# Attention operands and small sums rearranged between VectorE, ScalarE and GpSimd in a fused attention, MoE and FFN kernel

## The chip, the cores and the metric

The kernel runs on one core of one Trainium2 chip. The time is device microseconds of that core for one launch. A core has TensorE (PE, matmuls; its weight loads are shown as PEld), VectorE (DVE), ScalarE (ACT), GpSimd (POOL), SyncE (SP, which only issues transfers here) and 16 DMA engines. PE writes to PSUM; POOL works on SBUF alone.

## The reference, cut to what matters

Attention with a linear memory for B = 4 batches, H = 8 heads, S = 576 tokens and head size D = 64; its output feeds a top-1 mixture of 8 experts and then a dense FFN with ELU.

```python
scores = scale * (q @ k.T), causal, minus the row's maximum
a = exp(scores);  a /= a.sum(-1, keepdims=True) + 1e-9
local = a @ v
q_p = where(q > 0, q, exp(q) - 1) + 1
mem_out = (q_p @ M_prev) / ((q_p @ z_prev) + 1e-6)
g = 1 / (1 + exp(-beta))                       # one number per head
attn = g * mem_out + (1 - g) * local
logits = attn @ w_gate + modality_bias[modality_id]   # 2304 tokens x 8 experts
x = gate_w * (relu(attn @ w1[e]) @ w2[e])             # e: the expert with the largest logit
out = elu(x @ w_in) @ w_out
```

## The kernel before

The program is written against a tile framework: the order of the instructions on each engine is written out by hand, and the framework puts in the waits between engines from what each instruction reads and writes.

**Attention.** The 32 heads are done as 16 pairs p (four pairs a batch). A pair has NU = 7 units (L393): k = 0 is the last 64 tokens of both heads, k = 1 to 6 are tiles of 128 query rows of one head (two small tiles together in the last two units). For each unit, `scores` (L402) does the matmuls and a DVE pass (`low`, L399) that scales, masks and takes the row's minimum; one unit later `weights` (L437) takes the exponential on ACT (L447) with the row sum as a side result in `SUM[p]`; three units later PE transposes (`transposes`, L470), four later `evacuate` copies to SBUF (L482 on DVE, L480 on ACT). In unit 4 of the next pair come the products with V (`pv`, L507), `pv_tail` (L514, L515) and copies on ACT (L516, L517, L520). Two pairs on, in unit 0, `back` (L539) multiplies the result, which stands with head size on partitions, by the matrix `RH`: an identity for each head of the pair beside that head's rows of w_gate, so that one matmul turns the tile back to rows of tokens and gives its share of the gate's logits.

**Precision.** The score matmuls split q and k into a rounded high part and a low rest. `heads` holds three operands per pair. `prep_a` (L372, ACT) writes the rounded copy of q and of k to all 128 partitions; q and k were loaded twice, to partitions 0 to 63 and 64 to 127. `prep_b` (POOL) writes L = q - high (L378, 128 partitions) and overwrites one half of K, partitions 64 to 127, with k - high (L380). So K is [high; low] over the 128 contracted rows, Q is [high; high], and two matmuls, Q K and L K (L428, L429), give all four products. They are put for the next pair in units 0, 1, 3 and 4 (`PRE`): L378, L380, L378, L380, on POOL in that order with `fin` between.

**Small sums.** `tail_sums` (L529, DVE, unit 3) spreads the last tile's row sums over two columns with a mask `halves`; a small matmul in `pv_tail` gathers them. `row_scales` (L543, unit 5 of the next pair) makes (1 - g) / (sum + 1e-9) in three DVE steps (L548, L549, L550). `scaled` (L557) multiplies the output of `back` by it, `mem` (L581 to L583) does the memory part, and `fin` (L608, POOL; L606 on DVE from pair FINV = 13 on) adds the two: four adds a pair, of which two, for the last 64 tokens, are on partitions 0 to 63 for even batches and 64 to 127 for odd ones. The sums of the gate's part go to LX and LT.

**The order on DVE.** Small DVE steps do not stand in the written order. They lie in two queues, `steps` and `slow`; `pump` (L355), called behind each of the larger DVE instructions (L399, L482, L385, L389), takes one from `steps` and advances `slow` once. `drain` empties `steps` ahead of `back` and `mem`. Routing of a batch (`logits`, `route_a` to `route_c`, L611 to L714) lies in `slow`: it starts at pair 5, 9 and 13 for batches 0 to 2, with L614, which sums LX over the heads. The routed positions are scattered to a table in DRAM by POOL's indirect DMAs (`route_d`, L716, with the helper of L91 and L92), one per tile of 128 tokens, put at unit 4 of a later pair. Behind the third batch's scatters SP loads the first expert's indices (L897), POOL gathers its rows (L899), and the experts begin.

`omg` is 1 - g per head (L333), made by a `slow` step in pair 0. `mem_gate` (L313, units 0 and 1 of pair 1) multiplies the memory by the w_gate columns of RH.

Of the kernel before, what the change touches and what calls it, by code (L numbers as in the profile page):

```python
# [10 lines left out]
F32 = mybir.dt.float32  # L11
# [3 lines left out]
AF = mybir.ActivationFunctionType  # L15
ALU = mybir.AluOpType
# [12 lines left out]
DL = D + E  # L29
# [25 lines left out]
FINV = 13  # L55
# [47 lines left out]
def attention_memory_moe_ffn_kernel(  # L103
# [82 lines left out]
    with tc.tile_pool(name="ps", bufs=2, space=PSUM) as ps, ExitStack() as keep:  # L186
        for tag, n in (("s", 3), ("t", 2), ("po", 1), ("d", 2)):
            setattr(G, tag, lambda nm, tag=tag, n=n: ps.tile([128, 512], F32, tag=tag, bufs=n, name=nm))
        G.kp = keep.enter_context(G.pool("keep"))
        define_experts(tc, G)  # L190
        with G.pool("att") as ap, G.pool("hd", "right") as hd:
            attention(tc, G, ap, hd)
        ypool = ctx.enter_context(G.pool("yp", "right"))
        G.y = ypool.tile([128, 4, YW], F32, name="y")
        with G.pool("moe") as mp:
            experts(tc, G, mp)
# [4 lines left out]
def attention(tc, G, ap, hd):  # L201
    nc, wk = tc.nc, G.wk
# [11 lines left out]
    mm0, mod64, mt, lt0, halves = [k2[:, a:b] for a, b in ((0, 720), (720, 848), (848, 912), (912, 976), (976, 978))]  # L214
# [17 lines left out]
    RH = k1[:, o : o + 8 * DL].rearrange("p (k j d) -> p k j d", k=4, j=2)  # L232
# [51 lines left out]
    omg = ct("omg", [128, H])  # L284
# [39 lines left out]
            nc.vector.tensor_tensor(bd[r, :, j, D + 1 :].rearrange("p (b k) e -> p b k e", b=B), d[r, :, j].rearrange("p (b k) e -> p b k e", b=B), gj.unsqueeze(1).unsqueeze(3).to_broadcast([64, B, H // 2, E]), op=ALU.mult)  # L324


    def small_consts():
        nc.scalar.activation(g, bt, AF.Exp, scale=-1.0)
        nc.vector.tensor_scalar(g, g, 1.0, None, op0=ALU.add)
        yield  # L330
        nc.vector.reciprocal(g, g)
        yield
        nc.vector.tensor_scalar(omg, g, -1.0, 1.0, op0=ALU.mult, op1=ALU.add)  # L333
        yield
        for b in range(B):
            for j in range(2):
                r = slice(64 * j, 64 * j + 64)
                m = bd[r, 4 * b : 4 * b + 4, j, 1 : D + 1]
                nc.gpsimd.tensor_tensor(m, m, g[r].rearrange("p (h j) -> p h j", j=2)[:, :, j].unsqueeze(2).to_broadcast([64, H // 2, 64]), op=ALU.mult)
                yield  # L340
        nc.vector.tensor_copy(midf, mids.bitcast(I32).rearrange("p (t w) -> p t w", w=2))
        yield
        for m, dst in ((0, bm), (1, bm1)):
            nc.vector.tensor_scalar(midf[:, :, 1], midf[:, :, 0], float(m), None, op0=ALU.is_equal)
            yield
            nc.vector.tensor_tensor(dst, midf[:, :, 1:2].to_broadcast([128, NT, E]), mbs[:, m : m + 1, :].to_broadcast([128, NT, E]), op=ALU.mult)
            yield
        nc.vector.tensor_tensor(bm, bm, bm1, op=ALU.add)
        yield


    steps, slow = deque(), deque()
# [15 lines left out]
    def ops_of(p):  # L368
        return heads[:, p % 2, 0], heads[:, p % 2, 1], heads[:, p % 2, 2]
# [4 lines left out]
    def prep_b(p, j, r, eng=nc.gpsimd):  # L374
        qd, kd = LDT[p % 2][0:2]
        Q, K, L = ops_of(p)
        if r == 0:
            eng.tensor_tensor(L[:, j], qd[:, j, 0:512], Q[:, j].bitcast(F32), op=ALU.subtract)  # L378
        else:
            eng.tensor_tensor(K[64:128, j], kd[64:128, j, 0:512], K[64:128, j].bitcast(F32), op=ALU.subtract)  # L380

    def prep_phi(p, r):
        q2, m = LDT[p % 2][2], QP[p % 2]
# [11 lines left out]
    SRT, MX, SUM, ST = {}, {}, {}, {}  # L395
# [129 lines left out]
    STL = {}  # L525

    def tail_sums(p):
        STL[p] = wk.tile([128, 2], F32, tag="st", name=f"st{p}")
        nc.vector.tensor_tensor(STL[p], SUM[p][:, 4, 0:1].to_broadcast([128, 2]), halves, op=ALU.mult)  # L529

    def back(p):
        b = p // 4
# [8 lines left out]
    RS = {}  # L541

    def row_scales(p):  # L543
        h0 = 2 * (p % 4)
        rs = RS[p] = wk.tile([128, 5, 2], F32, tag="rs", name=f"rs{p}")
        steps.extend(
            (
                lambda: nc.vector.tensor_scalar(rs, SUM[p], 1e-9, None, op0=ALU.add),  # L548
                lambda: nc.vector.reciprocal(rs, rs),  # L549
                lambda: nc.vector.tensor_tensor(rs, rs, omg[:, h0 : h0 + 2].unsqueeze(1).to_broadcast([128, 5, 2]), op=ALU.mult),  # L550
            )
        )

    def scaled(p, d, a0, a1):
        k = a1 - a0
# [3 lines left out]
    def head_end(p):  # L559
        steps.extendleft(  # L560
            (
                lambda: fin(p),
                lambda: scaled(p, DB[p], 3, 5),
                lambda: scaled(p, DA[p], 0, 3),
            )
        )
# [20 lines left out]
    def fin(p):  # L587
        b, hp = p // 4, p % 4
        xs, xt = XS[b % 2], XT[b // 2]
        if hp == 0:  # L590
            nc.gpsimd.memset(xs[:, :, DM + 1 : ROW], 0.0)
            if b % 2 == 0:
                nc.gpsimd.memset(xt[:, DM + 1 : ROW], 0.0)
        c0 = 128 * hp
        mm, ol = MM[p % 2], OL[p % 2]
        r = 64 * (b % 2)
        hs = slice(2 * hp, 2 * hp + 2)
        half = slice(r, r + 64)
        for out, rows, c, d in (
            (xs[:, :, c0 : c0 + 128].rearrange("p c (j d) -> p c j d", d=64), slice(0, 128), slice(0, 4), slice(0, D)),  # L600
            (xt[half, c0 : c0 + 128].rearrange("p (j d) -> p j d", d=64), half, 4, slice(0, D)),
            (LX[:, :, hs], slice(0, 128), slice(0, 4), slice(D, DL)),
            (LT[b // 2][half, hs], half, 4, slice(D, DL)),
        ):
            if p >= FINV:
                steps.append(lambda out=out, rows=rows, c=c, d=d: nc.vector.tensor_tensor(out, mm[rows, c, :, d], ol[rows, c, :, d], op=ALU.add))  # L606
            else:
                nc.gpsimd.tensor_tensor(out, mm[rows, c, :, d], ol[rows, c, :, d], op=ALU.add)  # L608
# [158 lines left out]
    def put(p, k, f, *a):  # L767
        beside.setdefault(NU * p + k, []).append((f, a))

    for p in range(NP):  # L770
# [12 lines left out]
        else:  # L783
            put(p, ML[0], mem, p, 0, 3, s)
            put(p, ML[1], mem, p, 3, 5, s)
        put(p, 3, tail_sums, p)
        put(p + 1, RSC, row_scales, p)
        put(p + 2, 0, back, p)
        put(p + 2, 0, head_end, p)
        put(p, PHI, prep_phi, p, 0)  # L790
        put(p, PHI + 1, prep_phi, p, 1)
        if p + 1 < NP:
            for n, (j, r) in enumerate(((0, 0), (0, 1), (1, 0), (1, 1))):
                k = PRE[n] if p else PRE0[n]
                put(p, k, prep_a, p + 1, j, r)
                put(p, k, prep_b, p + 1, j, r)
            put(p, 6, loadv, p + 1)
# [5 lines left out]
    for n, k in enumerate(MW):  # L803
        put(0, k, mem_gate, n)
    put(0, SMALL, slow.append, small_consts())
    put(1, 3, G.late_constants)
    for b in range(3):
        K = 4 + b % 2
        ts = [tile_of(b, c) for c in range(K)]
        p, k = 4 * b + 5, GK[b]  # L810
# [38 lines left out]
    def first_prep(j):  # L849
        for r in range(2):  # L850
            prep_a(0, j, r, nc.vector if r else nc.scalar)
            prep_b(0, j, r, nc.vector if r else nc.gpsimd)
# [632 lines left out]
```

## Time and profile before

| | us |
|---|---|
| three runs | 1003.69, 1004.15, 1006.15 |
| median | 1004.15 |
| the profiled execution | 1004.68 |
| its span, first to last instruction | 1003.0 |
| busy: PE, DVE, ACT, POOL | 890.0, 577.5, 494.2, 319.8 |

Times in the rows are from the start of the span. The attention ends near 270 us, the experts run to about 580 us, the FFN to the end. An instruction's duration on DVE or POOL includes time in which it has started but is held; PE's ends are modelled.

### The profile page before, as it was taken

Reading aid. Unit: us, or ns where it says so; the run is one execution under the profiler, and the core shown is the slowest. Engines: PE = TensorE matmul, PEld = TensorE weight load, DVE = VectorE, ACT = ScalarE, POOL = GpSimd, SP = SyncE. Lnnn points to the kernel's source line nnn. Section 1 sums busy time; section 2 is a strip of 40 time slices with the busy share of each in tenths; the row PEclk is TensorE's granted clock in tenths of the full one; section 3 lists DMA queues with packets and bytes.
Section 4 is the critical chain, followed back from the end, with each engine's and each line's share of the span. In section 5 each row is a group of like instructions: output and inputs, shape, how many; then the busy total and the mean of one; then the engine's idle time right before and its main releaser. Section 6 shows DMA issues by size and latency. Waiting matters only on the chain. (4 is left out here: it accounts for less than half of the span.)

```text
span 1003.0 us, 16466 instructions
## 1 busy us (share of the span) xinstructions
PE 890.0 (89%) x5944; PEld 793.7 (79%) x5944; DVE 577.5 (58%) x1363; ACT 494.2 (49%) x1136; POOL 319.8 (32%) x428
## 2 busy tenths in 40 slices
PE   7999797887656799979998669999999999999996
PEld 4777675666556699979998468999999999999995
DVE  6999886878565332234222359888654444644442
ACT  4777574665521221123221346666665566755553
POOL 5765464355334521000000023222232222322223
PEclk9999998998978899979999779999999999999998
DMA  9755374561815541024101024432010000100001
GB/s 207 183 135 143 83 187 74 137 140 65 181 35 156 57 167 46 22 61 149 29 24 24 26 88 137 157 126 85 1 64 1 1 1 1 64 1 1 1 1 64
DMA packets 34054, 78.30 MB, mean 78 GB/s; under 512 B 11536, under 2 KB 11664, under 8 KB 33936
## 3 DMA queue, kind: packets, MB, share of 16 engines
q1 hardware_dynamic: 28016, 62.61, 24.2%
q0 software_dynamic: 4832, 12.14, 3.9%
q10 hardware_dynamic: 1088, 2.10, 0.9%
q8 instruction: 60, 0.98, 0.5%
q14 instruction: 58, 0.48, 0.2%
HBM read 67.25 MB, written 9.58 MB: 77 GB/s over the span
## 5 line engine op out<-in xcount | busy, mean ns | idle before, releaser
L1339 POOL TENSOR_TENSOR gl<-eg,gh 128x384 fp32r<-128x384 f32 x86 | 94.2, 1095 | 275.5 <-PE fh L1320 187.1
L1350 PE MATMUL facc<-wl,gh 128*128 128x512 f32 x288 | 113.0, 392 | 1.0 <-POOL wl L1300 1.0
L1350 PE MATMUL facc<-wh,gl 128*128 128x512 f32 x288 | 113.2, 393 | 0.0
L1350 PE MATMUL facc<-wh,gh 128*128 128x512 f32 x288 | 112.0, 389 | 0.0
L940 PE MATMUL h<-xh,W 128*128 128x256 f32 x512 | 97.6, 293 | 15.4 <-issue 6.9
L959 PE MATMUL acc<-hs,W 128*128 128x256 f32 x864 | 107.0, 283 | 0.5 <-DVE xb L914 0.3
L1320 PE MATMUL fh<-yh,first_w 128*128 128x384 f32 x384 | 101.1, 345 | 6.7 <-ACT yh L1311 6.7
L959 PEld LDWEIGHTS acc<-hs,W 128*128 128x128 f32 x864 | 104.5, 190 | 0.8 <-DVE xb L914 0.5
L1327 ACT ACTIVATE er<-fh 128x384 f32<-128x384 f32 x96 | 47.2, 492 | 114.8 <-PE fh L1320 111.1
L1330 DVE SCALAR_TENSOR_TENSOR ee<-ee,er 128x384 f32<-128x384 f32 x48 | 27.9, 580 | 120.8 <-ACT er L1329 119.2
L940 PEld LDWEIGHTS h<-xh,W 128*128 128x128 f32 x512 | 83.2, 199 | 16.8 <-DVE hs L943 7.3
L899 POOL DMA_INDIRECT xb<-xd,gi x26 | 25.0, 960 | 201.5 <-ACT xh L924 78.6
L942 ACT ACTIVATE hs<-h 128x256 fp32r<-128x256 f32 x72 | 27.1, 384 | 106.3 <-PE h L940 84.7
L1320 PEld LDWEIGHTS fh<-yh,first_w 128*128 128x128 f32 x384 | 72.0, 193 | 9.0 <-ACT yh L1311 7.0
L940 PE MATMUL h<-xl,W 128*128 128x256 f32 x256 | 74.6, 291 | 0.0
L447 ACT ACTIVATE sr<-sr,mx 128x512 f32<-128x512 f32 (+3 forms) x96 | 53.7, 563 | 40.7 <-DVE mx L399 35.8
L943 DVE SCALAR_TENSOR_TENSOR hs<-h,hs 128x256 fp32r<-128x256 f32 x72 | 29.8, 422 | 63.5 <-ACT hs L942 62.5
L1320 PE MATMUL fh<-yh,wh 128*128 128x384 f32 x192 | 64.5, 336 | 0.9 <-DVE eg L1331 0.9
L1320 PE MATMUL fh<-yh,wl 128*128 128x384 f32 x192 | 64.4, 336 | 0.0
L1350 PEld LDWEIGHTS facc<-wl,gh 128*128 128x128 f32 x288 | 54.0, 188 | 11.7 <-POOL wl L1300 1.4
L482 DVE COPY aT<-t 128x512 f32<-128x512 f32 (+3 forms) x106 | 50.6, 485 | 22.1 <-PE t L470 22.0
L1350 PEld LDWEIGHTS facc<-wh,gl 128*128 128x128 f32 x288 | 54.0, 188 | 11.4
(348 smaller groups left out, 2170.2 us busy)
## 6 DMA issues: line engine op xcount, KB each, us to landing
lqk<-in_qk_dram SPq DMA_DIRECT2D x30, 576.0 KB
raw<-in_w_dram SPq DMA_DIRECT2D x20, 512.0 KB
fraw<-in_win_dram SPq DMA_DIRECT2D x14, 512.0 KB
fraw<-in_wout_dram SPq DMA_DIRECT2D x14, 512.0 KB
lq<-in_qT_dram SPq DMA_DIRECT2D x16, 320.0 KB
vt<-in_vP_dram SPq DMA_DIRECT2D x16, 320.0 KB
xd<-early_rows SPq DMA_DIRECT2D x2, 1032.0 KB
xd<-late_rows SPq DMA_DIRECT2D x2, 1032.0 KB
```

Of the source, the lines that this page charges most:

```text
L447: nc.scalar.activation(sr[:, o : o + W], sr[:, o : o + W], AF.Exp, scale=-1.0, bias=mx[:, r : r + 1], accum_out=SUM[p][:, i, j : j + 1])
L482: nc.vector.tensor_copy(dst, src)
L899: nc.gpsimd.indirect_dma_start(xb[:, h, :], None, xd[0:rows, :], bass.IndirectOffsetOnAxis(ap=gi[:, h : h + 1], axis=0))
L940: nc.tensor.matmul(hp, wt[:, k, 128 * f : 128 * f + 128], xt[:, k, :], start=(k == 0 and r == 0), stop=(k == 3 and r == 2))
L942: nc.scalar.activation(hh, hp, AF.Relu)
L943: nc.vector.scalar_tensor_tensor(hl, hp, 0.0, hh.bitcast(F32), op0=ALU.max, op1=ALU.subtract)
L959: nc.tensor.matmul(o, wt[:, f, 128 * dc : 128 * dc + 128], ht, start=(f == 0 and r == 0), stop=(f == FF // 128 - 1 and r == 2))
L1320: nc.tensor.matmul(hp, wt[:, k, :], xt[:, k, :], start=(k == 0 and r == 0), stop=(k == 3 and r == 2))
L1327: nc.scalar.activation(r, hp, AF.Relu, scale=-1.0)
L1330: nc.vector.scalar_tensor_tensor(e, e, 1.0, r, op0=ALU.add, op1=ALU.mult)
L1339: eng.tensor_tensor(gl, gg, gh.bitcast(F32), op=ALU.subtract)
L1350: nc.tensor.matmul(ACC[g][a], gt[:, c], wt, start=(f == 0 and r == 0), stop=(f == NF - 1 and r == 2))
```

## The change

K's low part goes to partitions 0 to 63, so that K is [low; high]; the matmuls are the same. The factor 1 - g is multiplied into RH once (`scale_rows`, in pair 1, unit 2) and no longer into the row scales. The tail sums and the addition of 1e-9 are ACT instructions in the written order, and only the reciprocal stays a DVE step. `fin`'s two adds on partitions 64 to 127 go to DVE steps for all pairs.

```diff
+    def scale_rows():
+        for j in range(2):
+            r = slice(64 * j, 64 * j + 64)
+            w = omg[r].rearrange("p (k j) -> p k j", j=2)[:, :, j].unsqueeze(2).to_broadcast([64, 4, DL])
+            nc.vector.tensor_tensor(RH[r, :, j], RH[r, :, j], w, op=ALU.mult)
...
-            eng.tensor_tensor(K[64:128, j], kd[64:128, j, 0:512], K[64:128, j].bitcast(F32), op=ALU.subtract)
+            eng.tensor_tensor(K[0:64, j], kd[0:64, j, 0:512], K[0:64, j].bitcast(F32), op=ALU.subtract)
...
-        nc.vector.tensor_tensor(STL[p], SUM[p][:, 4, 0:1].to_broadcast([128, 2]), halves, op=ALU.mult)
+        nc.scalar.activation(STL[p], halves, AF.Copy, scale=SUM[p][:, 4, 0:1])
...
     def row_scales(p):
-        h0 = 2 * (p % 4)
         rs = RS[p] = wk.tile([128, 5, 2], F32, tag="rs", name=f"rs{p}")
-        steps.extend(
-            (
-                lambda: nc.vector.tensor_scalar(rs, SUM[p], 1e-9, None, op0=ALU.add),
-                lambda: nc.vector.reciprocal(rs, rs),
-                lambda: nc.vector.tensor_tensor(rs, rs, omg[:, h0 : h0 + 2].unsqueeze(1).to_broadcast([128, 5, 2]), op=ALU.mult),
-            )
-        )
+        nc.scalar.activation(rs, SUM[p], AF.Copy, bias=1e-9)
+        steps.append(lambda: nc.vector.reciprocal(rs, rs))
...
-            if p >= FINV:
+            if p >= FINV or rows.start:
                 steps.append(lambda out=out, rows=rows, c=c, d=d: nc.vector.tensor_tensor(out, mm[rows, c, :, d], ol[rows, c, :, d], op=ALU.add))
...
+    put(1, 2, scale_rows)
```

## Rows read from the trace of the kernel before

**Rows 1.** Windows of 20 us: length; busy (count) of PE, PEld, DVE, ACT, POOL; clock; DMA
```profile
60.00:80.00 20.00, 19.25 (x184) 15.08 (x180) 18.21 (x56) 13.84 (x41) 10.08 (x10) 1.00 0.46 113
...
160.00:180.00 20.00, 13.80 (x106) 10.96 (x106) 15.81 (x52) 10.41 (x30) 12.37 (x17) 0.83 0.41 99
```

**Rows 2.** DVE's groups by line and shape, 0 to 340 us: busy us, mean ns
```profile
L529 DVE TENSOR_TENSOR st<-sum,small 128x2 f32<-128x2 f32 x16 | 13.5, 844 | 0.0
...
L548 DVE TENSOR_SCALAR rs<-sum 128x10 f32<-128x10 f32 x16 | 10.2, 636 | 0.0
...
L557 DVE TENSOR_TENSOR ol<-db,rs 128x288 f32<-128x288 f32 x16 | 7.2, 452 | 0.0
...
L550 DVE TENSOR_TENSOR rs<-rs,omg 128x10 f32<-128x10 f32 x16 | 4.5, 284 | 0.0
...
L549 DVE RECIPROCAL rs<-rs 128x10 f32<-128x10 f32 x16 | 3.2, 201 | 0.0
...
L674 DVE TENSOR_TENSOR r_rb<-r_rb,r_ps 128x8 f32<-128x8 f32 x18 | 2.9, 163 | 0.3
...
L606 DVE TENSOR_TENSOR late_rows<-mm,ol 64x128 f32<-64x128 f32 x2 | 0.6, 290 | 0.0
```

**Rows 3.** Timeline of one pair, 60 to 75 us: start us, us, engine, line
```profile
63.90 1.87 POOL L380 TENSOR_TENSOR heads<-lqk,heads 64x512 fp32r<-64x512 f32 x1 [3.48 <-ACT heads L372]
64.16 0.21 ACT L447 ACTIVATION_READ_ACCUMULATOR sr<-sr,mx 128x1 f32 x1
...
64.56 1.24 DVE L548 TENSOR_SCALAR rs<-sum 128x10 f32<-128x10 f32 x1
...
66.54 0.52 PE L470 MATMUL t<-ident,sr 128*128 128x128 f32 x3
...
68.05 0.55 DVE L482 COPY aT<-t 128x384 f32<-128x384 f32 x1
...
71.11 1.27 POOL L608 TENSOR_TENSOR early_rows<-small,ol 128x512 f32<-128x512 f32 x1
...
71.75 0.18 DVE L582 RECIPROCAL rn<-rn 128x6 f32<-128x6 f32 x1
...
72.81 1.69 DVE L529 TENSOR_TENSOR st<-sum,small 128x2 f32<-128x2 f32 x1
...
73.21 1.27 POOL L378 TENSOR_TENSOR heads<-lqk,heads 128x512 fp32r<-128x512 f32 x1
```

**Rows 4.** Waits, 0 to 340 us: total us, times, longest us
```profile
ACT sr L447 <- DVE mx L399: 35.8, 25, 5.8
...
DVE aT L482 <- PE t L470: 22.0, 16, 2.4
```

**Rows 5.** Timeline of POOL behind the scatters of the first and second batch
```profile
147.38 0.96 POOL L92 DMA_INDIRECT idreg<-tid,rpi  x1 [0.22 <-issue]
148.40 1.27 POOL L378 TENSOR_TENSOR heads<-lqk,heads 128x512 fp32r<-128x512 f32 x1
158.93 1.26 POOL L380 TENSOR_TENSOR heads<-lqk,heads 64x512 fp32r<-64x512 f32 x1 [9.26 <-DMA idreg<-tid,rpi]
...
226.15 1.27 POOL L380 TENSOR_TENSOR heads<-lqk,heads 64x512 fp32r<-64x512 f32 x1 [7.45 <-DVE rs L548]
```

**Rows 6.** Timeline of DVE in the two stalls
```profile
162.49 0.61 DVE L614 TENSOR_REDUCE lg<-late_rows 128x32 f32<-128x256 f32 x1 [5.05 <-POOL late_rows L608]
...
164.56 0.94 DVE L619 TENSOR_TENSOR lg<-lg,bm 128x40 f32<-128x40 f32 x1
...
229.47 0.61 DVE L614 TENSOR_REDUCE lg<-late_rows 128x32 f32<-128x256 f32 x1 [2.62 <-POOL late_rows L608]
```

**Rows 7.** ACT's groups by line and shape, 0 to 340 us: busy us, mean ns
```profile
L517 ACT COPY sum<-pt 128x2 f32<-128x2 f32 x16 | 2.7, 166 | 0.0
...
L328 ACT ACTIVATE g<-bt 128x8 f32<-128x8 f32 x1 | 0.2, 205 | 0.0
```

**Rows 8.** Waits of SP's own queue, 100 to 300 us: total us, times, longest us
```profile
SPq L897 <- DMA idreg<-tid,rpi: 18.6, 1, 18.6
```

## The prediction

> **What bounds the kernel now.** All edits lie in the attention stage, about the first quarter of the span, so I went past the shares of the whole span to windows of 20 us [rows 1]: from 60 to 80 us VectorE (DVE) is busy 18.21 of 20 us and TensorE (PE) 19.25; from 160 to 180 both fall, to 15.81 and 13.80. Busy does not mean working, and the groups by line show it [rows 2]: a DVE multiply of 128x2 elements (L529) takes 844 ns on average and an add on 128x10 (L548) 636 ns, while a reciprocal on the same 128x10 takes 201 ns. The timeline tells why [rows 3]: L529 starts at 72.81 and ends at 74.50, and POOL's L378 runs 73.21 to 74.48; L548 runs 64.56 to 65.80, POOL's L380 63.90 to 65.77. DVE's multiplies and adds with both inputs in SBUF, and its tensor_scalar from SBUF, are held until the running POOL instruction is over. The reciprocal L582 ran its 0.18 us inside POOL's L608 (71.11 to 72.38), so it is not held.
>
> What a held instruction costs depends on the place. L529 stands ahead of the stretch where PE does the previous pair's attention-times-V (L507). DVE catches up with PE once in each pair: `DVE aT L482 <- PE t L470` is 22.0 us in 16 waits [rows 4], and L529 is the last long DVE instruction ahead of it. L529 is thus under PE's cover. L548 comes right behind that catching-up, where DVE leads and TensorE and ScalarE wait for it (ScalarE 35.8 us in 25 waits [rows 4]): its 1.24 us are bare.
>
> The second thing is two stalls. Behind the idreg scatters of a batch, L378 (all 128 partitions) starts 0.06 us after the last scatter (147.38 + 0.96, then 148.40), but the next L380, on partitions 64 to 127, starts 9.26 us after L378 ended, and 7.45 us in the next batch [rows 5]. The first is put down to the landing of the scatters. The second is put down to DVE's L548, whose data L380 does not touch; it is the same place in the order, so I read it as the same wait, its last instant held by DVE, as DVE is by POOL above. In both, POOL's later adds (L608) come late, and DVE, which reduces what they write (L614), idles 5.05 and 2.62 us [rows 6]. L378 and L380 subtract the same kind of data of the same pair; what sets them apart is the partition they begin at. I read it so: the program orders a POOL instruction that begins at partition 64 behind all that POOL issued before, its DMAs included, and one from partition 0 not.
>
> **The change part by part.** The sum is made against the profiled execution, 1004.68 us (span 1003.0 and 1.7 around it), 0.5 above the median of the runs, 1004.15.
>
> *K as [low; high].* L380 has the same 64x512 shape on partitions 0 to 63; both take 1.26 to 1.27 when nothing is in the way [rows 5], so nothing there. What it removes is the two stalls. No POOL instruction from partition 64 on is then left behind a scatter, since the odd batches' adds leave POOL as well. DVE's 5.05 + 2.62 = 7.7 us go. In the first stall's wake a small add, L619, took 0.94 [rows 6], held by POOL's backlog, where an add of 128x8 takes 0.16 [rows 2]: 0.8 us more. Bounds: nothing (the wait is for something else) and 16.7, both of POOL's stalls whole (POOL itself leads).
>
> The Trainium skill speaks against this edit (Perfetto Trace Analysis, "GPSIMD Engine Instruction" and "DMA Instruction — SWDGE (GPSIMD)"): POOL is eight processors of 16 partitions each, each with a queue of its own, and numbers 0 and 1 build the scatters' descriptors. By this rule the new L380 would stand behind descriptor building and the old one would not. The row on L378, which uses all partitions and starts 0.06 us behind a scatter, does not show it; what the rule would make of the time is the first rival.
>
> *1 - g in the output matrix.* L550 goes: 16 times, 4.5 us [rows 2], bare like L548, for it follows two DVE instructions behind. Added is scale_rows once, two 64x288 multiplies: nearest row 128x288 at 452 ns [rows 2], 0.9 together; bounds 0.6 (two of 290 ns, 64x128) and 3.4 (each also held for a POOL instruction of 1.27). It must follow mem_gate's matmuls, but mem_gate's own DVE multiplies, just ahead of it, wait for the same matmuls. The output matmuls keep shape and number.
>
> *The add of 1e-9 on ScalarE.* L548 goes from DVE: 10.2 us [rows 2]. What is held behind L389 next? Copies from PSUM and the reciprocal, which POOL does not hold, so the wait does not move on. ScalarE gets 16 instructions between 166 ns (128x2) and 205 ns (128x8) [rows 7], 3 us in all, in a queue with room (13.84 of 20 busy [rows 1]). The wait added is the reciprocal's on ScalarE; behind it in DVE stand the score passes L399. ScalarE's slot is behind the L447 that ends at 64.37, so the add ends near 64.57; DVE would reach the reciprocal where L548 starts now, at 64.56 [rows 3]. That is no wait, but a close thing: 0, bounds 0 and 0.5 per pair, 8 in all.
>
> *Tail sums on ScalarE.* L529 goes: 13.5 us of DVE [rows 2], under PE's cover: I take 0. Much of the wait would move on as well: L385, next to read SBUF alone, would meet the same POOL instruction. Bounds 0 and 13.5. ScalarE's 16 new instructions, 3 us, use a value that ScalarE wrote itself.
>
> *Odd batches' tail adds on DVE.* Five pairs (4 to 7 and 12), two adds each, 64x128 at 290 ns and 64x16 near the 163 ns of a 128x8 add [rows 2]: 2.3 us. Both have two SBUF inputs and stand right behind fin's large POOL add (1.27 us [rows 3]), so they are held: from nothing to twice 1.27 per pair. I take 0.5 us per pair, since in three of the five pairs a routing step is held at that place already and they only take its turn: 2.3 + 2.5 = 4.8, bounds 2.3 and 15. POOL saves two small adds a pair, hidden under its own waits for ScalarE.
>
> Of L548 and L550, 14.7 us, not all reaches the end. In the pair shown DVE would be 1.4 us early, and its copy at 68.05 would come at 66.65, but PE's transposes for it start at 66.54 and take 0.52, to 67.06 [rows 3], behind PE's own work: 0.4 of 1.4 is lost. I keep 80%, 11.8; bounds 0 and 14.7.
>
> Sum: 11.8 + 7.7 + 0.8 - 0.9 - 4.8 = 14.6 us. Behind the attention the third batch's scatters start the chain that opens the expert stage: SyncE waits 18.6 us for their landing to load the indices [rows 8]. They are issued by DVE's pace, so all that follows moves up whole. 1004.7 - 14.6 = 990.1, and 989.5 against the median.
>
> **The rivals.**
> 1. *The stall stays.* L380 waits for the scatters for another reason than its partitions, or the low half's processors are busy with the descriptors until the landing. For it: the row names the landing. Against: L378, just ahead, does not wait. 8.5 us are lost: 998.6. The skill's rule of the two processors, above, ends here.
> 2. *PE covers all.* DVE's savings only lengthen its waits for PE, which is busy 19.25 of 20 us at 60 to 80 [rows 1]. Then 8.5 - 5.7 = 2.8 remain: 1001.9. Against: ScalarE's 35.8 us of waits for DVE [rows 4].
> 3. *L529 counts too.* If PE's stretch itself moves up and the wait does not pass to L385, up to 13.5 more: 976 to 985.
> 4. *Slower: the reciprocal waits for ScalarE.* The add is queued behind ScalarE's exponentials; if ScalarE comes late by w in each pair, DVE stands for 16w at L549. From w = 14.6 / 16 = 0.91 us the gain is gone; if ScalarE is late in each pair by as much as POOL is now at L548, 1.24 us [rows 3], the time is 1004.7 - 14.6 + 19.8 = 1009.9. Against: the two meet at 64.57 and 64.56, above, and ScalarE is idle a third of the time [rows 1].
>
> **How the numbers follow.** Forecast (985 to 994) 52%; rival 3, 20%; rival 1 (994 to 1000) 13%; rival 2 (1000 to 1003) 8%; rival 4, 5%; the remaining 2% are nothing at all. A difference under 0.3%, 3 us, can't be told from none here. Faster by more (under 1001.1): 52 + 20 + 13 + half of rival 2 = 89%; same 6%; slower 5%. The range 976 to 998.5 leaves out the tail of rival 1 and rivals 2 and 4.
>
> **What would show it.** In the changed profile L380's longest wait behind a scatter is ScalarE's copy and not idreg; L614's idle time goes from 7.7 to near 0; L529, L548 and L550 are gone from DVE, L549 stays near 201 ns with no idle time ahead of it; `DVE aT L482 <- PE t L470` grows above 22.0 us, by what L529 gave. The prediction is wrong if L380 still waits after the scatters, if L549 shows idle time released by ScalarE, or if the new adds take over 1 us each.

## The result, and the profile of the changed kernel

The changed kernel is slower: 1009.09 us (median of 16 runs, 1005.75 to 1015.33) against 1001.46 for the kernel before, run beside it (16 runs, 992.32 to 1008.43). The ratio is 1.0083, 95% interval 1.0056 to 1.0110. Forecast were 989.5 us and a range of 976 to 998.5. The profiled execution took 1008.62 us, its span 1006.7.

Much of what was forecast is there. Ordinary pairs (3 to 5, with no routing in them) are shorter. The timeline of VectorE in the first batch shows two steps of qp, one pair apart (start us, us, engine, line):

```profile
66.18 0.82 DVE L396 SCALAR_TENSOR_TENSOR qp<-lq,qp 128x640 f32<-128x640 f32 x1
79.05 0.82 DVE L396 SCALAR_TENSOR_TENSOR qp<-lq,qp 128x640 f32<-128x640 f32 x1
```

The pair takes 12.87 us; the same step of before (L389) started at 63.82 and 77.87, so a pair took 14.05. VectorE's groups by line and shape, 0 to 340 us (busy us, mean ns, idle before), answer [rows 2, 6]:

```profile
L392 DVE TENSOR_SCALAR qp<-lq 128x640 f32<-128x640 f32 x16 | 15.8, 989 | 0.0
...
L607 DVE TENSOR_TENSOR small<-mm,ol 64x16 f32<-64x16 f32 x2 | 5.9, 2939 | 0.1
...
L553 DVE RECIPROCAL rs<-rs 128x10 f32<-128x10 f32 x16 | 3.3, 206 | 0.0
...
L615 DVE TENSOR_REDUCE lg<-late_rows 128x32 f32<-128x256 f32 x4 | 2.5, 617 | 0.0
...
L331 DVE TENSOR_TENSOR late_rows<-late_rows,omg 64x288 f32<-64x288 f32 x2 | 0.9, 449 | 0.0
```

The reciprocal (L553) takes 206 ns with no idle time ahead of it, L615 (L614 before) idles no more, scale_rows (L331) takes 0.9 us. What does not fit is L607: two adds of 64x16 elements have a mean of 2939 ns. One of them took 5.71 us. GpSimd, VectorE and TensorE around it, from their timelines:

```profile
153.25 0.96 POOL L92 DMA_INDIRECT idreg<-tid,rpi  x1 [0.21 <-issue]
...
154.52 0.96 POOL L92 DMA_INDIRECT idreg<-tid,rpi  x1 [0.21 <-issue]
155.51 1.27 POOL L385 TENSOR_TENSOR heads<-lqk,heads 128x512 fp32r<-128x512 f32 x1
156.73 1.26 POOL L387 TENSOR_TENSOR heads<-lqk,heads 64x512 fp32r<-64x512 f32 x1
157.95 1.52 POOL L609 TENSOR_TENSOR late_rows<-mm,ol 128x512 f32<-128x512 f32 x2
159.44 1.25 POOL L385 TENSOR_TENSOR heads<-lqk,heads 128x512 fp32r<-128x512 f32 x1
```
```profile
153.97 0.29 DVE L607 TENSOR_TENSOR xt<-mm,ol 64x128 f32<-64x128 f32 x1
...
155.03 5.71 DVE L607 TENSOR_TENSOR small<-mm,ol 64x16 f32<-64x16 f32 x1
160.76 0.29 DVE L489 COPY aT<-t 128x128 f32<-128x128 f32 x1
```
```profile
161.60 0.39 PE L469 MATMUL t63b<-ident,late_rows 128*64 128x128 f32 x1 [6.66 <-DVE aT L489]
...
162.57 4.01 PE L514 MATMUL po<-aT,vt 128*64 128x128 f32 x28
```

L387 starts right behind the scatter and L385, as forecast ([rows 5] had 9.26 us there). But now GpSimd runs from the scatter to 160.69 without a gap, and the add that starts at 155.03 ends only then. TensorE, waiting for the copy queued behind it, idles 6.66 us, and then its attention-times-V matmuls take 4.01 us, where the same 28 took 2.39 in 15 of the 16 pairs before. Windows show why (length, busy time of PE, PEld, DVE, ACT, POOL, then the granted clock as a share of 2.4 GHz, DMA share, GB/s). First the whole stretch, then four pieces of it:

```profile
20.00:256.00 236.00, 202.78 (x1737) 163.19 (x1739) 184.94 (x639) 145.84 (x440) 121.84 (x178) 0.89 0.51 122
...
101.00:108.00 7.00, 5.55 (x37) 3.77 (x37) 3.73 (x15) 2.76 (x8) 1.28 (x1) 0.51 0.01 3
125.00:128.00 3.00, 3.00 (x24) 2.32 (x22) 1.94 (x9) 0.65 (x3) 0.76 (x1) 0.50 0.04 14
142.00:145.00 3.00, 3.00 (x21) 1.84 (x19) 1.03 (x5) 0.49 (x2) 0.60 (x1) 0.51 0.00 0
159.00:166.00 7.00, 4.40 (x29) 3.46 (x31) 4.70 (x13) 0.87 (x3) 1.70 (x3) 0.51 0.03 3
```

Over the whole 0.89 are granted, before it were 0.96; in the four pieces TensorE runs at 1.2 GHz. The groups of the attention-times-V matmuls, 95 to 256 us, carry it (busy us, mean ns):

```profile
L514 PE MATMUL po<-aT,vt 128*64 128x128 f32 x180 | 19.9, 373 | 0.0
...
L514 PE MATMUL po<-aT,vt 128*64 128x384 f32 x36 | 9.9, 640 | 0.0
...
L514 PE MATMUL po<-aT,vt 128*64 128x256 f32 x36 | 8.0, 535 | 0.0
```

That is 37.8 us against 26.7 before (278, 486 and 379 ns each). ScalarE and VectorE wait longer for TensorE, and GpSimd for ScalarE, in the waits, 0 to 340 us (total us, times, longest):

```profile
POOL heads L387 <- ACT heads L379: 66.4, 15, 8.9
...
ACT oT L523 <- PE pt L522: 44.2, 15, 5.4
DVE aT L489 <- PE t L477: 41.7, 17, 4.9
```

Before, these were 42.2, 30.2 and 22.0 us (the last in [rows 4]). The loss sits in few places. From one L396 to the next, pair 1 took 4.0 us more than before, pairs 6 to 9 13.7 more, pair 13 2.7 more, and the others 11.6 less in all, so that the first expert matmul starts at 299.3 us and not at 290.1. Pairs 6 to 9 are those in which the odd adds of pairs 4 to 7 run; those of pair 12 run in pair 14, and pair 13 has none.

Not every hold lasts until GpSimd pauses. The timelines of GpSimd and VectorE in pair 8 of the changed kernel:

```profile
136.31 1.27 POOL L387 TENSOR_TENSOR heads<-lqk,heads 64x512 fp32r<-64x512 f32 x1
137.54 1.59 POOL L609 TENSOR_TENSOR late_rows<-small,ol 128x512 f32<-128x512 f32 x2
```
```profile
137.33 1.62 DVE L607 TENSOR_TENSOR xt<-small,ol 64x128 f32<-64x128 f32 x1
```

This odd add missed the end of L387 at 137.58 us, but it ended at 138.95, while GpSimd's two adds ran one behind the other until 139.13.

### The profile page after: what moved, and what is told of

Same layout as the page of the kernel before. It is cut to its first block, busy times and chain, and to the rows that moved or that the text cites. A ratio compares the mean times of both kernels' runs of the same rounds, so it can differ in the third digit from the quotient of the medians.

```text
span 1006.7 us, 16377 instructions
## 1 busy us (share of the span) xinstructions
PE 897.9 (89%) x5944; PEld 802.5 (80%) x5944; DVE 569.2 (57%) x1327; ACT 497.3 (49%) x1168; POOL 317.2 (32%) x418
## 5 line engine op out<-in xcount | busy, mean ns | idle before, releaser
L942 PEld LDWEIGHTS h<-xh,W 128*128 128x128 f32 x512 | 84.4, 202 | 13.7 <-issue 6.8
L387 POOL TENSOR_TENSOR heads<-lqk,heads 64x512 fp32r<-64x512 f32 x30 | 44.8, 1492 | 66.8 <-ACT heads L379 66.4
L1352 PEld LDWEIGHTS facc<-wl,gh 128*128 128x128 f32 x288 | 54.0, 188 | 11.7 <-POOL wl L1302 1.4
```

The lines of the kernel that those rows point to most:

```text
L387: eng.tensor_tensor(K[0:64, j], kd[0:64, j, 0:512], K[0:64, j].bitcast(F32), op=ALU.subtract)
L942: nc.tensor.matmul(hp, wt[:, k, 128 * f : 128 * f + 128], xt[:, k, :], start=(k == 0 and r == 0), stop=(k == 3 and r == 2))
L1352: nc.tensor.matmul(ACC[g][a], gt[:, c], wt, start=(f == 0 and r == 0), stop=(f == NF - 1 and r == 2))
```

## The experiments

Each ratio is to runs of the kernel before made beside it, with its 95% interval. A difference between two kernels is that of their ratios, its uncertainty the root of the summed squares of the two half-widths, rounded up, and 0.01 is 10 us.

**One part undone at a time.** e1 takes the odd adds back to GpSimd, e2 K's low half back to partitions 64 to 127, e3 the small sums back to VectorE, e4 both of the first two.

```diff
 e1, e4
-            if p >= FINV or rows.start:
+            if p >= FINV:
 e2, e4
-            eng.tensor_tensor(K[0:64, j], kd[0:64, j, 0:512], K[0:64, j].bitcast(F32), op=ALU.subtract)
+            eng.tensor_tensor(K[64:128, j], kd[64:128, j, 0:512], K[64:128, j].bitcast(F32), op=ALU.subtract)
 e3
-        nc.scalar.activation(STL[p], halves, AF.Copy, scale=SUM[p][:, 4, 0:1])
+        nc.vector.tensor_tensor(STL[p], SUM[p][:, 4, 0:1].to_broadcast([128, 2]), halves, op=ALU.mult)
-        nc.scalar.activation(rs, SUM[p], AF.Copy, bias=1e-9)
-        steps.append(lambda: nc.vector.reciprocal(rs, rs))
+        steps.extend(
+            (
+                lambda: nc.vector.tensor_scalar(rs, SUM[p], 1e-9, None, op0=ALU.add),
+                lambda: nc.vector.reciprocal(rs, rs),
+            )
+        )
```

> The changed kernel with the odd batches' tail adds back on GpSimd. Theory A (the odd adds on VectorE are the loss: they stand behind GpSimd's instructions in pairs 6 to 9, TensorE idles, its clock falls and the attention-times-V stretch runs at half rate; those four pairs took 13.7 us more than before): the extra low-clock stretches between 95 and 185 us go, pairs 6 to 9 fall by about 13 us in all, a stall behind the scatters may come back for some of it; time 0.985 to 0.998 of before. Theory B (K from partition 0 makes GpSimd's queue gapless, and that is what starves VectorE): stays near 1.008. Theory C (TensorE's clock falls simply because VectorE and ScalarE run ahead of it): stays near 1.008.

> The changed kernel with K's low half back on partitions 64 to 127; the odd adds stay on VectorE. Theory A (odd adds on VectorE): the loss in pairs 6 to 9 stays and the wait behind the scatters comes back, 1.005 to 1.018 of before. Theory B (K from partition 0 starves VectorE): the holds of VectorE behind several GpSimd instructions go, 0.985 to 0.995. Theory C: about 1.008.

> The changed kernel with the tail sums and the add of 1e-9 back on VectorE (the 1 - g fold stays). Theory A or B: the 1.2 us that each ordinary pair gained go for the larger part and nothing comes back in pairs 6 to 9: 1.012 to 1.022 of before. Theory C (the clock falls because VectorE has too little to do, or ScalarE's new instructions are the cost): the clock holds and the time falls to 0.995 to 1.003.

> Only the 1 - g fold and the small sums on ScalarE; K and the odd adds as before. Theory A or B: ordinary pairs keep their 1.2 us each (16 pairs, 19 us at most), the start may lose 4 us, the stalls behind the scatters stay: 0.984 to 0.993 of before. Theory C: the clock falls here too, 1.000 to 1.010.

| kernel | median us | ratio | interval |
|---|---|---|---|
| e1 | 990.82 | 0.9893 | 0.9858 to 0.9927 |
| e2 | 998.01 | 0.9969 | 0.9948 to 0.9990 |
| e3 | 1015.62 | 1.0151 | 1.0113 to 1.0188 |
| e4 | 995.05 | 0.9933 | 0.9909 to 0.9958 |

The odd adds on VectorE cost 19.0 us ± 4.5 where K is [low; high] (changed kernel less e1), and 3.6 ± 3.3 where it is [high; low] (e2 less e4). So by the times neither theory A nor B is right alone: it takes both edits. Theory C falls, since moving the sums back costs 6.8 ± 4.7 more. e2 came out below theory A's range and above B's. How K's partition acts, e2 does not show: its odd adds in pairs 6 to 9 last 3.6 us in all (9.3 in the changed kernel), but the one of pair 9 is not held at all, as the timelines of GpSimd and VectorE show:

```profile
148.94 0.96 POOL L92 DMA_INDIRECT idreg<-tid,rpi  x1 [0.22 <-issue]
```
```profile
149.33 0.17 DVE L607 TENSOR_TENSOR small<-mm,ol 64x16 f32<-64x16 f32 x1
```

It starts 0.39 us into the last scatter, against 0.51 in the changed kernel. e1 shows in the timeline of GpSimd what [rows 5] were read for:

```profile
146.87 1.28 POOL L387 TENSOR_TENSOR heads<-lqk,heads 64x512 fp32r<-64x512 f32 x1
148.10 1.27 POOL L609 TENSOR_TENSOR late_rows<-mm,ol 128x512 f32<-128x512 f32 x1
154.81 0.45 POOL L609 TENSOR_TENSOR xt<-mm,ol 64x128 f32<-64x128 f32 x1 [5.44 <-DMA idreg<-tid,rpi]
```

Behind the same scatters the instructions that begin at partition 0 go at once, and the odd add, from 64 on, waits 5.44 us for the landing of data it does not use.

**TensorE's gaps filled.** w2 leaves the changed kernel as it is and adds transposes of the identity, read by nobody, ahead of the matmuls before which TensorE stood idle. w1 does it for e1 at the one gap at 15.7 us.

```diff
 w1, w2
+    def warm(u, n):
+        d = po_(f"warm{u}")
+        for i in range(n):
+            nc.tensor.transpose(d[:, 128 * (i % 4) : 128 * (i % 4) + 128], ident, ident)
...
+    for u, n in ((45, 12), (52, 15), (59, 17), (66, 46), (94, 24), (101, 14)):
+        put(0, u, warm, u, n)
 w1, in place of the last two lines
+    for u, n in ((5, 17),):
+        put(0, u, warm, u, n)
```

> The changed kernel with extra transposes of the identity on TensorE (12, 15, 17, 46, 24 and 14 of them, into the free accumulator) ahead of the transposes behind which it stood idle in pairs 6 to 9, 13 and 14. VectorE is held as before. Theory A (what a hold costs beyond itself is the clock): the low stretches at 101, 125, 142, 159, 227 and 248 us go, the attention-times-V stretches of 4.0 to 4.5 us return to 2.39, 6 to 10 us in all: 0.998 to 1.003 of before. Rival (the hold of VectorE alone is the cost): 1.006 to 1.012.

> The kernel of e1 with 17 extra transposes of the identity (into an accumulator that is still free, read by nobody) on TensorE ahead of the transposes that wait 2.5 us at 15.7 us; they leave the work itself alone. Theory A (a gap of TensorE lets its clock fall, and the clock is what costs): the 13.7 us at 0.50 from 18.8 us on go, pair 1 falls from 19.1 to about 15.5 us, the time falls by 3 to 4 us against e1, to 0.985 to 0.988 of before. Rival (the clock only mirrors a wait that is there anyway; pair 1 is long for another reason, scale_rows or ScalarE's new instructions): same as e1, 0.989, or 1 us slower for the extra work.

w2: 996.60 us, 0.9935 (0.9911 to 0.9958), 14.8 us ± 3.7 below the changed kernel, by nothing but work for an engine that had none. VectorE is held as before, and the windows, VectorE's timeline and TensorE's show what changed:

```profile
20.00:256.00 236.00, 215.15 (x1967) 176.55 (x1966) 196.18 (x676) 154.90 (x467) 130.20 (x188) 0.96 0.57 136
```
```profile
150.37 5.75 DVE L612 TENSOR_TENSOR small<-mm,ol 64x16 f32<-64x16 f32 x1
```
```profile
149.73 4.64 PE L507 MATMUL warm<-ident 128*128 128x128 f32 x41
...
156.99 0.27 PE L469 MATMUL t63b<-ident,late_rows 128*64 128x128 f32 x1 [1.69 <-DVE aT L489]
...
157.54 2.39 PE L519 MATMUL po<-aT,vt 128*64 128x128 f32 x28
```

The hold is 5.75 us, the attention-times-V stretch 2.39, the mean clock 0.96. The gain is more than theory A expected, and not all of it belongs to the odd adds: in the profiles pairs 6 to 9 are 7.3 us shorter than in the changed kernel, and pairs 13 and 14, in which no odd add is held, 4.2. Against e1 the changed kernel's pairs 6 to 9 are 17.3 us longer, and the odd adds on VectorE themselves last 9.3 us there. So of what they cost in these pairs about half is their own length and somewhat less than half TensorE's clock behind the gaps, an estimate from one profile of each kernel.

w1: 991.50 us, 0.9885 (0.9843 to 0.9927), no different from e1. The window from 24 to 33 us has a clock of 1.00, where e1 has 0.50 from 18.7 to 32.4, but pair 1 still took 20.0 us (19.1 in e1), with 0.66 granted from 19 to 24 us and 0.58 from 33 to 37. VectorE, GpSimd and TensorE in their timelines:

```profile
29.31 2.75 DVE L331 TENSOR_TENSOR late_rows<-late_rows,omg 64x288 f32<-64x288 f32 x2
```
```profile
29.03 1.27 POOL L385 TENSOR_TENSOR heads<-lqk,heads 128x512 fp32r<-128x512 f32 x1
30.27 1.47 POOL L387 TENSOR_TENSOR heads<-lqk,heads 64x512 fp32r<-64x512 f32 x1
```
```profile
32.93 0.27 PE L469 MATMUL t7b<-ident,late_rows 128*64 128x128 f32 x1 [2.56 <-DVE aT L489]
...
33.48 4.07 PE L519 MATMUL po<-aT,vt 128*64 128x128 f32 x28
```

On time, scale_rows ran into two GpSimd instructions, and the attention-times-V matmuls behind it took 4.07 us for 2.39; the wait had only moved.

**K mixed, scatters moved.** w4 puts K's low half at partition 64 in four pairs of the changed kernel. w3 and x1 move the scatters of e1.

```diff
 w4
-            eng.tensor_tensor(K[0:64, j], kd[0:64, j, 0:512], K[0:64, j].bitcast(F32), op=ALU.subtract)
+            r = slice(64, 128) if p in (7, 8, 9, 14) else slice(0, 64)
+            eng.tensor_tensor(K[r, j], kd[r, j, 0:512], K[r, j].bitcast(F32), op=ALU.subtract)
 w3
-SY = 4
+SY = 6
 x1
-        for r in range(1, 4):
+        for r in range(4 if b == 0 else 1, 5 if b == 0 else 4):
             put(p + r, SY, put_scatters)
```

> The changed kernel with K's low half on partitions 64 to 127 in pairs 7, 8, 9 and 14 alone (their work on GpSimd lies in pairs 6, 7, 8 and 13). Theory A (the odd adds cost as much as they do because GpSimd's instructions follow each other without a gap where they stand): the holds of the odd adds at 121.1 and 137.3 us shrink, pairs 6 to 8 give back 4 to 9 us, pair 9 and its hold of 5.5 us stay: 0.998 to 1.004. Rival (the partition of K matters only behind the scatters): 1.006 to 1.011.

> The kernel of e1 with each batch's scatters issued two steps later in their pair (SY 6 for 4), so that the odd batch's adds on partitions 64 to 127 stand ahead of the first batch's scatters on GpSimd and not behind them. If an instruction from partition 64 on is what is ordered behind the scatters' landing (e1 has one such wait, 5.44 us at 154.81), the wait goes and with it VectorE's 2.70 us and the low clock at 158.7 us: 3 to 5 us less than e1, 0.984 to 0.987. If it waits for GpSimd's queue in general: 0.989.

> The kernel of e1 with the first batch's four scatters one pair later, behind the last odd batch's adds on partitions 64 to 127 (in w3 they had moved ahead by a pair, and the wait with them). If those adds are ordered behind the scatters' landing, the 5.44 us wait at 154.81 us goes, VectorE's 2.70 us of idle time goes, and TensorE's gap of 2.65 us and the 3.4 us at 0.50 behind it: 2 to 4 us less than e1, 0.985 to 0.988 of before. If the wait is for the queue and not for the landing: 0.989.

w4: 996.96 us, 0.9946 (0.9920 to 0.9972), better than theory A expected, but not for its reason alone: the hold in pair 9 that was to stay is gone. Its timelines of GpSimd and VectorE:

```profile
148.02 0.95 POOL L92 DMA_INDIRECT idreg<-tid,rpi  x1 [0.21 <-issue]
149.04 1.28 POOL L385 TENSOR_TENSOR heads<-lqk,heads 128x512 fp32r<-128x512 f32 x1
```
```profile
148.40 0.17 DVE L608 TENSOR_TENSOR small<-mm,ol 64x16 f32<-64x16 f32 x1
```

The add starts 0.38 us into the last scatter and takes 0.17 us; in the changed kernel it starts 0.51 us into it and takes 5.71. So w4, like e2, does not tell whether K's partition shortens such a hold.

w3: 995.07 us, 0.9927 (0.9901 to 0.9954), a miss. The scatters, ready since pair 8, went out ahead of the adds at 127.8 us and not later, and an odd add waited 6.43 us for their landing again. x1: 991.36 us, 0.9901 (0.9868 to 0.9934), the same as e1. The 5.44 us wait is gone, and the hold of the changed kernel is back on another instruction, a routing step, as the timeline of VectorE and the waits of TensorE, 150 to 168 us, show:

```profile
158.36 5.57 DVE L646 TENSOR_TENSOR r_oh<-r_fm,revE 128x40 f32<-128x40 f32 x1
```
```profile
PE t70b L469 <- DVE rn L583: 6.2, 1, 6.2
```

Without a wait behind the scatters GpSimd runs from 158.00 to 163.87 us without a gap, here too. A VectorE instruction with two SBUF inputs that falls there can be the one, odd add or not.

**scale_rows later, and no fold.** x2 is w1 with scale_rows three units later, x3 is x1 and x2 together, x4 is e1 with 1 - g multiplied in each pair again and no scale_rows.

```diff
 x2, x3
-    put(1, 2, scale_rows)
+    put(1, 5, scale_rows)
 x4
-    put(1, 2, scale_rows)
...
+        h0 = 2 * (p % 4)
         steps.append(lambda: nc.vector.reciprocal(rs, rs))
+        steps.append(lambda: nc.vector.tensor_tensor(rs, rs, omg[:, h0 : h0 + 2].unsqueeze(1).to_broadcast([128, 5, 2]), op=ALU.mult))
```

> The kernel of w1 (e1 with the gap at 15.7 us filled) with scale_rows three steps later, under the attention-times-V matmuls of pair 1, where VectorE waits 3.6 us for TensorE. In w1 its two multiplies took 2.75 us behind GpSimd (L331, 29.31), TensorE idled 2.53 us and the next stretch took 4.07 us for 2.39. If that is what makes pair 1 long: pair 1 falls from 20.0 to 15.5 to 16.5 us and the time by 3 to 4 us, to 0.984 to 0.986 of before. If pair 1 is long for another reason: 0.988 to 0.989.

> x1 and x2 together: K as [low; high], the fold, the sums on ScalarE, the odd adds on GpSimd ahead of the scatters, the start filled and scale_rows later. If both costs are as the traces show them they add up: 0.980 to 0.984 of before. If what one gives is lost in the next wait for TensorE or a transfer: 0.985 to 0.989.

> The kernel of e1 without the fold: 1 - g is multiplied in VectorE again behind the reciprocal (16 of the old L550) and scale_rows is gone. If the fold is worth the 4.5 us of L550 bare and scale_rows costs 1: 3 us slower than e1, 0.992. If L550 lies under a wait and scale_rows costs the 1 to 3 us that its row shows: the same as e1 or 2 us faster, 0.987 to 0.989.

x2: 986.23 us, 0.9857 (0.9811 to 0.9903), the fastest here and below both kernels, though not measurably below e1. Pair 1 falls to 15.8 us, what it was before the change; pair 2 takes 15.0 for 12.9, since TensorE's output matmuls now wait 1.7 us for scale_rows. x3: 988.52 us, 0.9882 (0.9838 to 0.9925); the two do not add up. x4: 989.70 us, 0.9889 (0.9844 to 0.9934): without the fold the time is 0.4 us ± 5.7 below e1's, so the fold is worth nothing that shows. In the profiles an ordinary pair takes 13.3 us without it and 12.9 with it; what it gives there is lost again elsewhere.

**Pair 7 alone.** y1 is the changed kernel with the odd adds of pair 7, which run in pair 9, back on GpSimd; y2 is e1 with those alone on VectorE.

```diff
 y1
-            if p >= FINV or rows.start:
+            if p >= FINV or (rows.start and p != 7):
 y2
+            if p >= FINV or (rows.start and p == 7):
```

> The changed kernel with the odd adds of pair 7 alone back on GpSimd (they run in pair 9, behind the first batch's scatters, where the one of 5.71 us stood); those of pairs 4, 5, 6 and 12 stay on VectorE. If most of the 19 us that the odd adds cost on VectorE is this one hold and what TensorE loses behind it: 0.990 to 0.996 of before. If it is spread over the pairs 6 to 8 and 13, whose holds are 1.6 us or less: 1.000 to 1.006.

> The kernel of e1 with the odd adds of pair 7 alone on VectorE, the complement of the run before. If the one hold is the cost: 0.997 to 1.004 of before, with an add of over 5 us in pair 9. If it is spread over the other pairs: 0.985 to 0.991, less than e1 by the 5.44 us wait of GpSimd that goes. If the add starts a little earlier against the scatters it is not held at all (0.17 us, as in w4), and the time is that of e1 or up to 4 us less.

y1: 999.31 us, 0.9975 (0.9952 to 0.9998); y2: 998.24 us, 0.9966 (0.9941 to 0.9991), with the hold back:

```profile
146.20 5.52 DVE L607 TENSOR_TENSOR small<-mm,ol 64x16 f32<-64x16 f32 x1
```

Pair 7's adds cost 10.8 us ± 3.6 (changed kernel less y1) or 7.3 ± 4.3 (y2 less e1), and those of pairs 4, 5, 6 and 12 11.7 ± 3.8 or 8.2 ± 4.2. It is about half and half: both expectations were half right.

## Why the prediction was wrong

**The step that failed** is "Odd batches' tail adds on DVE", 4.8 us with bounds 2.3 and 15; it measured 19.0 ± 4.5. The forecast of 14.6 us faster became 7.6 slower (1009.09 less 1001.46), a miss of 22, and this term holds 14 of it; the rest lies in the sums and in K, below. Two things were wrong in it:
- *How long a hold lasts.* I bounded it by "twice 1.27 per pair", one GpSimd instruction for each add, as I had read each hold of [rows 3] to end with the running one. The add of pair 9 lasted 5.71 us, through five. [rows 3] already spoke against it: L529 begins at 72.81 us, 0.40 ahead of L378, and ends with L378 at 74.50. What held it first are two small adds in GpSimd's timeline of before, which follow at once:

```profile
72.76 0.31 POOL L608 TENSOR_TENSOR late_rows<-small,ol 128x64 f32<-128x64 f32 x1
73.03 0.22 POOL L608 TENSOR_TENSOR small<-small,ol 64x16 f32<-64x16 f32 x1
```

  My own step on K took the wait of 9.26 us [rows 5] out of GpSimd's queue just there, and I added up the two edits as if they were independent. That the pause would have ended this hold is argued and not shown: in e2 and w4 it did not begin. For it speaks e1, where VectorE's L392, begun at 146.98 us behind the same scatters, took 2.75 us and ended behind GpSimd's L609 (148.10 and 1.27), where GpSimd paused.
- *What it costs.* I priced a hold at its own length. The ten odd adds last 9.8 us in all in the changed kernel, which is inside the bounds of 2.3 and 15; 19.0 is not. The prediction has no term for TensorE's clock, though [rows 1] show 1.00 and 0.83 in two windows of the attention. TensorE idled 1.62 us until 100.58, 2.22 until 124.11, 2.46 until 140.76 and 6.66 until 161.60, and then ran the pieces at 1.2 GHz shown above; these meet the attention-times-V matmuls, behind which ScalarE and VectorE wait. w2 gives back 14.8 us with the holds in place, by its profile 7.3 of them in pairs 6 to 9.

On the clock the Trainium skill (TensorE: Matmul & The Clock Gate, "Why this matters for your kernels") advises against idle gaps of TensorE between bursts of matmuls. w2 agrees: 0.96 granted for 0.89.

**The other terms.** *The sums on ScalarE and the fold*: 11.8 - 0.9 = 10.9 us were forecast, e4 has 6.7 ± 2.5. In ordinary pairs the forecast holds: L548 (1.24 us) and L550 (0.16) are 1.4 us there, and 1.2 a pair arrive, a little over the 80% that I kept. L529's wait moved on to L392 (L385 before; 989 ns on average, 480 where it is free), and the rest of it into VectorE's wait for TensorE, both as I had it, so rival 3 is not borne out. The timelines of VectorE in one pair, before and then changed:

```profile
66.59 0.16 DVE L550 TENSOR_TENSOR rs<-rs,omg 128x10 f32<-128x10 f32 x1
76.35 0.69 DVE L482 COPY aT<-t 128x512 f32<-128x512 f32 x1 [0.81 <-PE t L470]
```
```profile
74.52 1.28 DVE L392 TENSOR_SCALAR qp<-lq 128x640 f32<-128x640 f32 x1
77.53 0.69 DVE L489 COPY aT<-t 128x512 f32<-128x512 f32 x1 [1.64 <-PE t L477]
```

Most of what e4 lacks it loses at the start, by its profile: pair 1 took 19.1 us for 15.8. The reciprocal never waits for ScalarE: rival 4 has the right side by the wrong mechanism, and that its 1009.9 us lies beside the measured 1009.09 is luck. *scale_rows*: 0.9 us in the profile, its value to the digit, where nothing held it, and 2.75 in w1, inside its bounds. That pair 1 became 4.0 us longer has two parts. TensorE came 0.5 us earlier to a wait for data and idled 2.31 us (1.81 before), and the 13.7 us from 19.2 us on ran at 1.2 GHz; with that gap filled (w1), scale_rows stood in the way. x2, which meets both, has the 15.8 us of before.

*K as [low; high]*: the reading of the partitions was right (e1's rows above), and no L387 waits for idreg. The 8.5 us forecast for it have no run of their own; without the odd adds on VectorE it brings 4.0 ± 4.3 (e1 less e4), with them it costs 11.4 ± 3.5 (changed kernel less e2).

Against rival 1, the Trainium skill's rule (Perfetto Trace Analysis, "DMA Instruction — SWDGE (GPSIMD)") that two of GpSimd's processors build the descriptors made nothing wait here: L387 on partitions 0 to 63 starts 1.22 us after L385, itself 0.03 us behind the last scatter.

**What stays open.** When a hold ends between two GpSimd instructions that follow at once and when it does not, and when a scatter holds an add: the rows show both ways of each. Why pair 13, in which no odd add runs, took 18.9 us in the changed kernel and 13.8 in e1. And with the clock in play a single profile of each kernel gives the places, not their exact shares.

## What to carry to other kernels

An instruction that another engine's queue can hold may be held through several instructions of that queue, so an edit that takes the pauses out of the queue must be priced together with every instruction that it can hold. Where TensorE sits on the chain, price a wait at its length plus what the granted clock does behind it; idle stretches filled with matmuls nobody reads gave back 14.8 us here. Undo one part at a time and one pair of parts: the odd adds on VectorE cost 3.6 ± 3.3 us where K was left alone and 19.0 ± 4.5 where it was not, and e1, the same change less one line, beats both kernels at 0.9893.

## What the runs showed of the hardware

A VectorE add with two SBUF inputs can be held by GpSimd for far longer than one of its instructions takes: 5.71, 5.75 and 5.52 us in three kernels, through a scatter's end and five instructions each until GpSimd paused, and a routing step 5.57 us in x1 through nine. The Trainium skill (SBUF — State Buffer, "SBUF: two separate sides") says that whichever of the two starts first has the shared ports for the whole instruction. The rows go beyond it: the end of one GpSimd instruction was no opening there, where the next followed at once.

Elsewhere it was one. The add at 137.33 us of the changed kernel got in between two adds of GpSimd, and in w1 the first multiply of scale_rows between L385 and L387, which took 1.47 us for 1.27. In e3 the odd add at the place of the 5.71 us got in after 4.26, between GpSimd's last two.

Nor is an add always held by a scatter. One that started 0.72 us into the third scatter (changed kernel, 153.97 us) took 0.29 us, one 0.38 us into the last (w4) 0.17; those 0.51 (changed kernel, w2) and 0.70 us (y2) into the last were held.
